# Second layer of a fused attention and two-MLP kernel in blocks of four token tiles, and a padded copy of U's columns for the shared tile

## Chip, cores and metric

One core of one Trainium2 chip. The metric is the device time in microseconds (us) of one execution; three timed runs of the kernel before gave 1811.48 us in the median (1806.88 to 1813.13). All times below are us unless marked ns.

## What is computed

Three stages on float32 data with 8 batches, 576 tokens and 512 channels. In short form:

```python
x = attention(q, k, v)              # per head, in chunks of 64 tokens
x = x + relu(layernorm(x) * g_ln @ w1_a) @ w2_a        # first layer, 512 -> 2048 -> 512
u = x + transpose(transpose(x) @ U @ V)                # along the tokens: U is 576x32, V is 32x576
out = u + relu(u @ w1_b) @ w2_b                        # second layer, 512 -> 2048 -> 512
```

The MLP matrices, U and V arrive as float64; the kernel turns them into float32 parts itself.

## The kernel before, in words

The 8 x 576 = 4608 tokens are 36 tiles of 128 (`NT`). A batch is four and a half tiles long, so every ninth tile is shared: of tiles 9k to 9k+8, the one with `r = i % 9 == 4` holds 64 tokens of batch 2k and 64 of batch 2k+1.

**Blocks and steps.** Both layers work on blocks of `TPB = 3` tiles (`BT = 384` tokens): blocks 0 to 11 are the first layer, 12 to 23 the second. A block has `NF = 16` steps, one for each slice of 128 of the 2048 hidden channels; `seq` (line 652) lists all 384 pairs (block, slice) in order. In the main loop (lines 806 to 829) step `g` issues `g1` of pair `g`, then whatever the dictionary `plan` holds for that step, then `g2` of pair `g - 2` (`LAG = 2`). Each engine executes its own instructions in that order.

**g1** (line 602) makes one slice of the hidden layer: 12 matmuls into one PSUM bank `h0` or `h1` (4 slices of the input channels, and for each the products high by high, high by low, low by high of a split number format). The weight slice, 128x128, is the stationary operand; the transposed activations `xh`, `xl` are the moving one, 384 columns wide. ScalarE writes the relu's high part `hh` (line 613), VectorE its remainder `hl` (line 614), each to a ring of three buffers.

**g2** (line 617) adds that slice into the outputs: for each tile of the block 3 matmuls, with `hh` or `hl` as stationary operand and 512 columns of `w2` moving, into the tile's own bank `acc0` to `acc2`. After the last slice `finish` (line 629) adds the residual on VectorE, and `store` writes the tiles out four steps later.

**Preparation.** While one block is computed, `plan` prepares the next. For a tile of the second layer: `u_load` (SP queue) reads the first layer's result back, `st_U` adds the low-rank part (one matmul, or two for a shared tile, and a VectorE add), `st_US` and `gather` move it through DRAM with DMAs of the ACT queue, `st_UE` transposes it on VectorE, rounds it on ScalarE (`xh`) and takes the remainder on GpSimd (`xl`). The three tiles start at offsets 0, 4 and 8 in the steps of the block before; `z_load`, `z_sum`, `z_rep` prepare a batch's low-rank factor ahead of its first tile.

**Low-rank sums.** `z_mm` (line 531) multiplies the finished tile `i` of the first layer by U's rows for it. The 32 result rows go to one of four groups of 32 PSUM partitions (`grp = r % 4`, `r = i % 9`) of the bank `z`. Line 539 lets a shared tile use 64 of its rows for one batch and the other 64 for the next, by two calls. The sums of a block's tiles are issued together, at most in two places: blocks with a shared tile issue part 0 at one step and part 1 three steps later. `ut` holds U's rows in 9 columns of tiles; its column 4 has rows 512 to 575 of U on top and rows 0 to 63 below.

**Order around the change.** U is loaded at step 27 (`load_ut`), V at step 175 (`load_vst`: 8 DMAs on SP, then conversion on ScalarE and VectorE). Block 11 runs from step 176 to 191, the second layer from step 192. During block 11 `w_back` and `w_split` replace the weights.

Of the kernel before, what the change touches and what calls it, by code (L numbers as in the profile page):

```python
# [18 lines left out]
def fused_kernel(ctx, tc, q, k, v, g_ln, w1_a, w2_a, U, V, w1_b, w2_b, out):  # L19
    nc = tc.nc  # L20
# [8 lines left out]
    TPB = 3  # L29
    BT = TPB * P  # L30
    NB = NT // TPB
    KT = DM // P
    NF = DFF // P
    LAG = 2
# [4 lines left out]
    const = ctx.enter_context(tc.tile_pool(name="const", bufs=1))  # L39
    wp = ctx.enter_context(tc.tile_pool(name="wp", bufs=1))  # L40
    rawp = ctx.enter_context(tc.tile_pool(name="rawp", bufs=3))
    xtp = ctx.enter_context(tc.tile_pool(name="xtp", bufs=2))
    hp_ = ctx.enter_context(tc.tile_pool(name="hp", bufs=3))
    xp = ctx.enter_context(tc.tile_pool(name="xp", bufs=7))
    qkp = ctx.enter_context(tc.tile_pool(name="qkp", bufs=1))
    t1 = ctx.enter_context(tc.tile_pool(name="t1", bufs=1))
# [16 lines left out]


    ident = const.tile([P, P], F32, name="ident")
    gbc = const.tile([P, DM], F32, name="gbc")
    ut = const.tile([P, 9, RK], F32, name="ut")
    nhalf = const.tile([P, 1], F32, name="nhalf")

    x1_d = [dr.tile([P, DM], F32, name=f"x1d{i}") for i in range(NT)]  # L70
# [129 lines left out]
    def load_ut():  # L200
        Ui = U.bitcast(I32)
        raw = raw_tile()
        v = raw.rearrange("p (t r) w -> p t (r w)", r=RK)
        nc.sync.dma_start(out=v[:, 0:4], in_=Ui[0:512].rearrange("(t p) r -> p t r", p=P))
        nc.sync.dma_start(out=v[0:64, 4], in_=Ui[512:576])
        nc.sync.dma_start(out=v[64:128, 4], in_=Ui[0:64])
        nc.sync.dma_start(out=v[:, 5:9], in_=Ui[64:576].rearrange("(t p) r -> p t r", p=P))
        o = ut.rearrange("p t r -> p (t r)")
        a, c = conv_f32(raw, P, 9 * RK, o)
        nc.vector.tensor_tensor(out=c, in0=c, in1=a, op=ALU.mult)  # L210
        nc.vector.tensor_tensor(out=o, in0=o, in1=c, op=ALU.add)

    def load_vst():
        Vi = V.bitcast(I32)
        vst = qkp.tile([P, S + 2 * CH], F32R, tag="kt", name="vst")
        zs["V"] = vst
        nc.gpsimd.memset(f32(vst[:, 0:CH]), 0.0)
        nc.gpsimd.memset(f32(vst[:, CH + S:]), 0.0)
        n = S // 2
        for h in range(2):  # L220
            raw = raw_tile()
            for m in range(4):
                nc.sync.dma_start(out=raw.rearrange("p a w -> p (a w)")[32 * m:32 * m + 32, :2 * n], in_=Vi[:, 2 * n * h:2 * n * (h + 1)])
            o = vst[:, CH + n * h:CH + n * (h + 1)]
            a, c = conv_f32(raw, P, n, o)
            for m in (1, 3):
                pp = slice(32 * m, 32 * m + 32)
                nc.vector.tensor_tensor(out=o[pp], in0=c[pp], in1=a[pp], op=ALU.mult)
# [239 lines left out]
    def st_N(i):  # L468
# [9 lines left out]
        else:  # L478
            nc.vector.tensor_scalar(out=xn, in0=x, scalar1=mv[:, 0:1], scalar2=rs, op0=ALU.subtract, op1=ALU.mult)  # L479
            nc.gpsimd.tensor_tensor(out=xn, in0=xn, in1=gbc, op=ALU.mult)  # L480

    def xt_tile(j, t):
        if t == 0:
            xt[j] = (xtp.tile([P, KT, BT], F32R, tag="xh", name="xh"), xtp.tile([P, KT, BT], F32R, tag="xl", name="xl"))
        return (a[:, :, t * P:(t + 1) * P] for a in xt[j])

    def st_E1(i):
        src = state.pop(("n", i)).rearrange("p (k c) -> p k c", k=KT)
# [42 lines left out]
    def z_mm(i, part):  # L531
        r = i % 9
        b = 2 * (i // 9) + part
        grp = r % 4
        first = r in ((0, 1, 2, 3) if part == 0 else (4, 5, 6, 7))
        last = r in ((4, 1, 2, 3) if part == 0 else (8, 5, 6, 7))
        if b not in zst:
            zst[b] = psp.tile([P, DM], F32, tag="z", name="zps")
        pp = slice(0, P) if r != 4 else slice(64 * part, 64 * part + 64)
        mm(zst[b][32 * grp:32 * grp + 32, :], ut[pp, r, :], xs[i][pp, :], start=first, stop=last)  # L540

    def z_out(b):
        z4 = t1.tile([P, DM], F32, tag="xn" if b == B - 1 else "cvd", name="z4")
# [27 lines left out]
    us = {}  # L571

    def u_load(i):
        x1 = xp.tile([P, DM], F32, tag="x", name="x1")
        nc.sync.dma_start(out=x1, in_=x1_d[i])
        us[i] = x1

# [15 lines left out]
        spread(NT + i, us[i])  # L593

    def st_UE(i):
        split(NB + i // TPB, i % TPB, state.pop(("w", NT + i)), "xn")


    ht = {}
    acc = {}  # L600

    def g1(j, f):
        xh, xl = xt[j]
        wh, wl = (a.rearrange("p (k f) -> p k f", k=KT) for a in wt[0, f])
        ps = ps_tile("h", [P, BT])
        n = 0
        for kk in range(KT):
            for l, r in ((wh, xh), (wh, xl), (wl, xh)):
                mm(ps, l[:, kk], r[:, kk, :], start=n == 0, stop=n == 3 * KT - 1)
                n += 1  # L610
        hi = hp_.tile([P, BT], F32R, tag="hh", name="hh")
        lo = hp_.tile([P, BT], F32R, tag="hl", name="hl")
        nc.scalar.activation(out=hi, in_=ps, func=AF.Relu)  # L613
        nc.vector.scalar_tensor_tensor(out=lo, in0=ps, scalar=0.0, in1=f32(hi), op0=ALU.max, op1=ALU.subtract)  # L614
        ht[j, f] = (hi, lo)

    def g2(j, f):
        hi, lo = ht.pop((j, f))
        wh, wl = wt[1, f]
        for t in range(TPB):  # L620
            if f == 0:
                acc[j, t] = psp.tile([P, DM], F32, tag=("h1", "m1", "z")[t] if j == 1 else f"acc{t}", name="acc")
            tt = slice(t * P, (t + 1) * P)
            a = acc[j, t]
            mm(a, hi[:, tt], wh, start=f == 0, stop=False)
            mm(a, hi[:, tt], wl, start=False, stop=False)
            mm(a, lo[:, tt], wh, start=False, stop=f == NF - 1)

    def finish(j):
        for t in range(TPB):  # L630
            i = j % NB * TPB + t
            x = xs[i] if j < NB else us[i]
            nc.vector.tensor_tensor(out=x, in0=acc.pop((j, t)), in1=x, op=ALU.add)  # L633

    def store(j):
        for t in range(TPB):
            i = j % NB * TPB + t
            if j < NB:
                nc.sync.dma_start(out=x1_d[i], in_=xs[i])
            else:  # L640
                nc.sync.dma_start(out=out[i * P:(i + 1) * P, :], in_=us.pop(i))


    with tc.manual_schedule():
# [7 lines left out]
        seq = [(0, f) for f in range(LEAD)]  # L652
        for f in range(NF):
            seq += [(1, f)] + [(0, f + LEAD)] * (f + LEAD < NF)
        seq += [(j, f) for j in range(2, 2 * NB) for f in range(NF)]
        pos = {x: n for n, x in enumerate(seq)}

        for n in range(2, 2 * NB):
            g = NF * (n - 1)
            ends = []  # L660
            for t in range(TPB):
                i = (n % NB) * TPB + t
                s = g + 4 * t
                if n == 2:
                    s = (10, 15, 24)[t]
                    at(s - 6, load_qk_nat, i)
# [39 lines left out]
            if 2 <= n < NB - 1:  # L706
                parts_ = 4 if n < 4 else 9
                for part in range(parts_):
                    at(g + {2: 12, 3: 8, 4: 4}.get(n, 3) + part, load_qk, n + 1, part, parts_)
        for n in range(2 * NB):  # L710
            g = pos[n, NF - 1] + 1
            at(g + LAG + 2, store, n)
            if n < NB:
                g = max(g, pos[1, NF - 1] + 1)
                both = any((n * TPB + t) % 9 == 4 for t in range(TPB))
                early_z = []
                for t in range(TPB):
                    i = n * TPB + t
                    r = i % 9
                    if r <= 4:  # L720
                        early_z.append((z_mm, (i, 0)))
                    if r == 4:
                        at(g + 5, z_out, 2 * (i // 9))
                    if r >= 4:
                        plan.setdefault(g + (6 if both else 3), []).insert(0, (z_mm, (i, 1)))
                    if r == 8:
                        at(g + 5, z_out, 2 * (i // 9) + 1)
                z_first[g + 3] = z_first.get(g + 3, []) + early_z
# [5 lines left out]
        for p in range(len(EARLY), NP):  # L734
            at(max(p - 4, 2), weight, p)
        at(27, load_ut)
        at(NF * (NB - 2) + 15, load_vst)
        PRE_G = 58
        for p in range(NP):
            g = PRE_G + p * 7 // 2  # L740
# [65 lines left out]
        for g in range(len(seq) + LAG + 3):  # L806
            if g < pos[1, 0] + LAG:
                banks.update(h=("h0", "m0"), m=("m1", "h1", "z"))
            elif g < 10:
                banks.update(h=("h0", "m0"), m=())  # L810
            elif g <= pos[0, NF - 1] + LAG:
                banks.update(h=("h0",), m=("m0",))
            elif g == pos[0, NF - 1] + LAG + 1:
                banks.update(h=("h0",), m=("m0", "acc1", "acc2"))
            elif g < 2 * NF:
                banks.update(h=("h0", "acc0"), m=("m0", "acc1", "acc2"))
            elif g <= 2 * NF + 1:
                banks.update(h=("h0",), m=("m0",))
            else:
                banks.update(h=("h0", "h1"), m=("m0", "m1"))  # L820
            if g < len(seq):
                g1(*seq[g])
            for fn, a in plan.get(g, ()):
                fn(*a)
            if LAG <= g < len(seq) + LAG:
                j, f = seq[g - LAG]
                g2(j, f)
                if f == NF - 1:
                    finish(j)
# [24 lines left out]
```

## Time and profile before

| what | value |
|---|---|
| median of three timed runs | 1811.48 us |
| lowest and highest | 1806.88 and 1813.13 us |
| the profiled execution's own time | 1808.26 us |
| its span in the trace | 1806.5 us |
| mean granted TensorE clock | 0.985 |
| TensorE busy with matmuls | 1747.0 us |
| DMA traffic | 167.57 MB |

The span is the time from the first to the last instruction that the trace shows; 1.8 us lie around it. PE stands for TensorE's matmuls, PEld for its weight loads, DVE for VectorE, ACT for ScalarE, POOL for GpSimd, SP for the queue that issues most DMAs. Matmuls overlap in the pipeline, so the duration of one is longer than the distance to the next; rates below are taken from distances between starts. A busy share near 100% says that the engine is never without work, not that each piece of it is as short as it can be.

### The profile page before, as it was taken

How to read it: one execution, taken by the hardware profiler on the slowest of the kernel's cores; microseconds unless marked ns; L12 is line 12 of the kernel's file. 1: busy time of each engine (PE TensorE's matmuls, PEld its weight loads, DVE VectorE, ACT ScalarE, POOL GpSimd, SP SyncE). 2: the span in 40 equal slices, each digit the busy share in tenths (PEclk: the TensorE clock that was granted, in tenths of full speed). 3: DMA queues.
4: the chain of work that ended last, by engine and by line, in shares of the span. 5: the costliest groups of instructions: out<-in, count | busy, mean ns of one | idle time of the engine just before them, and what ended most of it. 6: DMA issues, size and time to landing. Idle time of an engine off the chain costs nothing.

```text
span 1806.5 us, 26695 instructions
## 1 busy us (share of the span) xinstructions
PE 1747.0 (97%) x10536; PEld 1538.9 (85%) x10536; DVE 790.3 (44%) x1544; ACT 381.5 (21%) x714; POOL 183.3 (10%) x196
## 2 busy tenths in 40 slices
PE   6899898999999999999999999999999999999999
PEld 4778777888788888888889899999999999999998
DVE  6898643466566656556545221221221221221211
ACT  4333311122222222212124111111111111111110
POOL 1000001111011120111211001010001001010000
PEclk8899999999999999999999999999999999999999
DMA  7344324546365463554345221220221121220100
GB/s 170 100 125 109 78 70 97 131 118 155 104 149 138 110 169 108 144 149 115 110 132 175 65 65 41 65 76 24 77 70 42 59 65 41 65 76 24 53 30 18
DMA packets 293101, 167.57 MB, mean 93 GB/s; under 512 B 189424, under 2 KB 251888, under 8 KB 292976
## 3 DMA queue, kind: packets, MB, share of 16 engines
q1 hardware_dynamic: 212048, 93.48, 20.2%
q10 hardware_dynamic: 80928, 72.39, 14.1%
q8 instruction: 83, 1.36, 0.3%
q14 instruction: 42, 0.34, 0.1%
HBM read 112.82 MB, written 52.95 MB: 92 GB/s over the span
## 4 chain that ended last, share of the span: by engine, by line
PE 85%; DVE 7%; DMA 3%; issue 2%; ACT 1%; SPq 1%; POOL 1%; ACTq 0%; DVEq 0%; POOLq 0%
PE psh L59 41%; PE acc L59 40%; PE psm L59 2%; PE zps L59 1%; DVE hl L614 1%; DMA raw<-in_moe_w_ch 1%; DVE cvt L94 1%; DVE cvt L102 1%; ACT hh L613 1%; DMA k<-in_k 0%; DMA q<-in_q 0%; DMA nat<-in_k 0%; SPq L282 0%; DVE cvt L93 0%; DVE cvt L103 0%
## 5 line engine op out<-in xcount | busy, mean ns | idle before, releaser
L614 DVE SCALAR_TENSOR_TENSOR hl<-psh,hh 128x384 fp32r<-128x384 f32 x384 | 213.6, 556 | 876.0 <-ACT hh L613 875.4
L59 PE MATMUL psh<-xh,w0h 128*128 128x384 f32 x1536 | 522.1, 340 | 16.0 <-DVE hl L614 12.9
L59 PE MATMUL psh<-xh,w0l 128*128 128x384 f32 x1536 | 521.2, 339 | 1.0 <-DVE w0l L146 1.0
L59 PE MATMUL psh<-xl,w0h 128*128 128x384 f32 x1536 | 519.3, 338 | 1.1 <-DVE xl L498 0.9
L59 PE MATMUL acc<-w1h,hh 128*128 128x512 f32 x1152 | 459.2, 399 | 4.9 <-DVE x L633 4.0
L59 PE MATMUL acc<-w1l,hh 128*128 128x512 f32 x1152 | 456.2, 396 | 0.0
L59 PE MATMUL acc<-w1h,hl 128*128 128x512 f32 x1152 | 455.6, 395 | 0.0
L613 ACT ACTIVATE hh<-psh 128x384 fp32r<-128x384 f32 x384 | 188.8, 492 | 1121.9 <-PE psh L59 947.7
L59 PEld LDWEIGHTS psh<-xh,w0h 128*128 128x128 f32 x1536 | 291.4, 190 | 37.2 <-DVE hl L614 16.4
L59 PEld LDWEIGHTS psh<-xl,w0h 128*128 128x128 f32 x1536 | 290.9, 189 | 18.0 <-DVE xl L498 1.3
L59 PEld LDWEIGHTS psh<-xh,w0l 128*128 128x128 f32 x1536 | 290.6, 189 | 1.4 <-DVE w0l L146 1.4
L59 PEld LDWEIGHTS acc<-w1h,hh 128*128 128x128 f32 x1152 | 217.2, 189 | 50.3 <-ACT hh L613 7.7
L59 PEld LDWEIGHTS acc<-w1h,hl 128*128 128x128 f32 x1152 | 216.8, 188 | 48.1
L59 PEld LDWEIGHTS acc<-w1l,hh 128*128 128x128 f32 x1152 | 216.9, 188 | 36.9
L520 POOL TENSOR_TENSOR xl<-wT,xh 128x512 fp32r<-128x512 f32 x63 | 81.3, 1290 | 941.0 <-ACT xh L519 937.3
L460 POOL TENSOR_SCALAR rs<-mv 128x1 f32<-128x1 f32 x36 | 8.8, 244 | 537.6 <-DVE mv L458 529.4
L519 ACT CAST xh<-wT 128x512 fp32r<-128x512 f32 x63 | 39.4, 625 | 89.1 <-DVE wT L517 89.1
L633 DVE TENSOR_TENSOR x<-acc,x 128x512 f32<-128x512 f32 x72 | 45.2, 681 | 3.7 <-PE acc L59 3.7
L517 DVE STREAM_TRANSPOSE wT<-w 128x512 f32<-128x512 f32 x63 | 44.3, 703 | 5.6 <-DMA wd<-v_pl 2.3
L480 POOL TENSOR_TENSOR xn<-xn,gbc 128x512 f32<-128x512 f32 x27 | 35.8, 1327 | 41.9 <-DVE xn L479 34.0
L59 PEld LDWEIGHTS psm<-kt_pl,qt 64*64 64x64 f32 x1056 | 20.3, 145 | 17.5 <-issue 13.3
L59 PE MATMUL psm<-kt_pl,qt 64*64 64x64 f32 x1056 | 24.9, 237 | 8.7 <-DVE kt_pl L300 7.5
(99 smaller groups left out, 924.0 us busy)
## 6 DMA issues: line engine op xcount, KB each, us to landing
w<-sp ACTq DMA_DIRECT2D x90, 256.0 KB, 2.7
x1d<-x SPq DMA_DIRECT2D x36, 256.0 KB, 2.5
x<-x1d SPq DMA_DIRECT2D x36, 256.0 KB, 3.1
sp<-x ACTq DMA_DIRECT2D x144, 64.0 KB, 1.8
out<-x SPq DMA_DIRECT2D x36, 256.0 KB, 2.1
v_pl<-in_v SPq DMA_DIRECT2D x132, 64.0 KB, 2.8
raw<-in_moe_w_ch SPq DMA_DIRECT2D x64, 128.0 KB, 2.9
raw<-in_moe_w_ch SPq DMA_DIRECT2D x16, 512.0 KB, 3.5
```

The source lines that it names most:

```text
L59: nc.tensor.matmul(o, lhsT=l, rhs=r, start=start, stop=stop)
L94: nc.vector.scalar_tensor_tensor(out=bi, in0=hw, scalar=-0x40000000, in1=bi, op0=ALU.bitwise_and, op1=ALU.bitwise_or)
L102: nc.vector.scalar_tensor_tensor(out=c, in0=d, scalar=2.0 ** -20, in1=c, op0=ALU.mult, op1=ALU.add)
L460: nc.gpsimd.tensor_scalar(out=rs, in0=mv[:, 1:2], scalar1=1e-6, scalar2=None, op0=ALU.add)
L480: nc.gpsimd.tensor_tensor(out=xn, in0=xn, in1=gbc, op=ALU.mult)
L517: nc.vector.transpose(out=x.rearrange("p k (a j) -> p a k j", a=4), in_=w.rearrange("p a (k i) -> p a k i", k=KT))
L519: nc.scalar.copy(out=hi, in_=x)
L520: nc.gpsimd.tensor_tensor(out=lo, in0=x, in1=f32(hi), op=ALU.subtract)
L613: nc.scalar.activation(out=hi, in_=ps, func=AF.Relu)
L614: nc.vector.scalar_tensor_tensor(out=lo, in0=ps, scalar=0.0, in1=f32(hi), op0=ALU.max, op1=ALU.subtract)
L633: nc.vector.tensor_tensor(out=x, in0=acc.pop((j, t)), in1=x, op=ALU.add)
```

## The change

The second layer gets blocks of its own: `TP2 = 4` tiles, 9 blocks of 16 steps instead of 12. Its `g1` matmuls have 512 moving columns in place of 384, its `g2` runs 12 matmuls in place of 9. The fourth accumulator is the bank `m1` in the first of these blocks (in which other work then has `m0` alone) and `z` in the others. The preparation offsets are 0, 4, 6, 8. The activation buffers and the hidden rings of the first layer become parts of one tile `act`; from block 11 on the rings lie in the buffers `q6` and `k6`, which attention no longer needs. A block's fourth residual tile goes alternately to the buffers `cvd` and `gbc`.

`ut` gets a tenth column: GpSimd copies the lower half of column 4 to it and writes zeros to its upper half and to the lower half of column 4, so that both calls for a shared tile use all 128 rows. V's DMAs are issued at step 169 and its conversion at 173.

```diff
+    TP2 = 4
+    NB2 = NT // TP2
...
-    xtp = ctx.enter_context(tc.tile_pool(name="xtp", bufs=2))
-    hp_ = ctx.enter_context(tc.tile_pool(name="hp", bufs=3))
+    actp = ctx.enter_context(tc.tile_pool(name="actp", bufs=1))
...
-    gbc = const.tile([P, DM], F32, name="gbc")
-    ut = const.tile([P, 9, RK], F32, name="ut")
+    gbc = t1.tile([P, DM], F32, tag="gbc", name="gbc")
+    ut = const.tile([P, 10, RK], F32, name="ut")
...
+        nc.gpsimd.memset(ut[0:64, 9], 0.0)
+        nc.gpsimd.tensor_copy(out=ut[64:128, 9], in_=ut[64:128, 4])
+        nc.gpsimd.memset(ut[64:128, 4], 0.0)
...
+    act = actp.tile([P, 2 * 2 * KT * BT + 6 * BT], F32R, name="act")
+
+    def tiles_of(j):
+        return [j * TPB + t for t in range(TPB)] if j < NB else [(j - NB) * TP2 + t for t in range(TP2)]
...
+            n = KT * P * len(tiles_of(j))
+            o = (2 * n * ((j - NB) % 2)) if j >= NB else (2 * n + 3 * BT) * (j % 2)
+            xt[j] = tuple(act[:, o + m * n:o + (m + 1) * n].rearrange("p (k c) -> p k c", k=KT) for m in range(2))
...
+    def h_tiles(j, f):
+        n = BT if j < NB else TP2 * P
+        if j < NB - 1:
+            m = 2 * KT * BT
+            r = hpos[j, f] % 3
+            return (act[:, o + r * BT:o + (r + 1) * BT] for o in (2 * m + 3 * BT, m))
+        if not hring:
+            for nm in ("q6", "k6"):
+                hring[nm] = qkp.tile([P, 3, TP2 * P], F32R, tag=nm, name="h" + nm[0])
+        return (hring[nm][:, hpos[j, f] % 3, :n] for nm in ("q6", "k6"))
...
-        pp = slice(0, P) if r != 4 else slice(64 * part, 64 * part + 64)
-        mm(zst[b][32 * grp:32 * grp + 32, :], ut[pp, r, :], xs[i][pp, :], start=first, stop=last)
+        mm(zst[b][32 * grp:32 * grp + 32, :], ut[:, 9 if r == 4 and part else r, :], xs[i], start=first, stop=last)
...
-        x1 = xp.tile([P, DM], F32, tag="x", name="x1")
+        j, t = divmod(i, TP2)
+        x1 = xp.tile([P, DM], F32, tag="x", name="x1") if t < 3 else t1.tile([P, DM], F32, tag=("cvd", "gbc")[j % 2], name="x1")
...
-        ps = ps_tile("h", [P, BT])
+        ps = ps_tile("h", [P, len(tiles_of(j)) * P])
...
-        for t in range(TPB):
+        for t in range(len(tiles_of(j))):
             if f == 0:
-                acc[j, t] = psp.tile([P, DM], F32, tag=("h1", "m1", "z")[t] if j == 1 else f"acc{t}", name="acc")
+                tag = f"acc{t}" if t < 3 else ("m1" if j == NB else "z")
+                acc[j, t] = psp.tile([P, DM], F32, tag=("h1", "m1", "z")[t] if j == 1 else tag, name="acc")
...
-        seq += [(j, f) for j in range(2, 2 * NB) for f in range(NF)]
+        seq += [(j, f) for j in range(2, NB + NB2) for f in range(NF)]
...
-                s = g + 4 * t
+                s = g + (0, 4, 6, 8)[t]
...
-        at(NF * (NB - 2) + 15, load_vst)
+        at(NF * (NB - 2) + 9, load_V)
+        at(NF * (NB - 2) + 13, make_vst)
...
-                banks.update(h=("h0", "h1"), m=("m0", "m1"))
+                banks.update(h=("h0", "h1"), m=("m0",) if pos[NB, 0] + LAG - 1 <= g <= pos[NB, NF - 1] + LAG else ("m0", "m1"))
```

## Rows read from the trace of the kernel before

**Rows 1.** The page: busy time of the engines; shares of the chain that ended last.

```profile
PE 1747.0 (97%) x10536; PEld 1538.9 (85%) x10536; DVE 790.3 (44%) x1544; ACT 381.5 (21%) x714; POOL 183.3 (10%) x196
...
PE 85%; DVE 7%; DMA 3%; issue 2%; ACT 1%; SPq 1%; POOL 1%; ACTq 0%; DVEq 0%; POOLq 0%
```

**Rows 2.** Busy time by stretch: PE, PEld, DVE, ACT, POOL; granted clock, DMA share, GB/s.

```profile
130.00:400.00 270.00, 252.16 (x1666) 216.13 (x1665) 159.26 (x329) 64.61 (x119) 22.93 (x28) 0.97 0.41 101
400.00:900.00 500.00, 493.03 (x3560) 425.89 (x3559) 303.97 (x612) 112.56 (x207) 73.16 (x84) 1.00 0.51 132
900.00:1000.00 100.00, 99.86 (x489) 86.42 (x490) 51.74 (x86) 33.49 (x66) 11.79 (x11) 1.00 0.48 154
1000.00:1800.00 800.00, 800.00 (x4008) 723.27 (x4002) 168.34 (x293) 117.32 (x229) 65.31 (x51) 1.00 0.17 52
```

**Rows 3.** What PE waited for from 400 us on: us, times, longest.

```profile
PE psm L59 <- DVE kt_pl L300: 3.6, 2, 2.1
PE acc L59 <- DVE x L633: 2.4, 2, 1.5
```

**Rows 4.** Timeline of PE, three steps of the second layer: start, duration.

```profile
1201.97 0.33 PE L59 MATMUL psh<-xh,w0h 128*128 128x384 f32 x1
...
1203.04 0.33 PE L59 MATMUL psh<-xh,w0h 128*128 128x384 f32 x1
...
1204.08 0.39 PE L59 MATMUL acc<-w1h,hh 128*128 128x512 f32 x1
...
1206.16 0.33 PE L59 MATMUL psh<-xh,w0h 128*128 128x384 f32 x1
...
1214.53 0.33 PE L59 MATMUL psh<-xh,w0h 128*128 128x384 f32 x1
```

**Rows 5.** Timeline of PE: the last 18 matmuls, first and last of them.

```profile
1798.18 0.39 PE L59 MATMUL acc<-w1h,hh 128*128 128x512 f32 x1
...
1802.04 0.39 PE L59 MATMUL acc<-w1h,hl 128*128 128x512 f32 x1
```

**Rows 6.** Timeline of PE: two low-rank sums, one of a shared tile.

```profile
942.44 2.02 PE L59 MATMUL zps<-x,ut 128*32 128x512 f32 x4
944.39 0.50 PE L59 MATMUL psm<-zs,vst 128*128 128x512 f32 x1
```

**Rows 7.** Timeline of PE: three low-rank sums, none of a shared tile.

```profile
999.77 1.06 PE L59 MATMUL zps<-x,ut 128*32 128x512 f32 x6
1000.76 0.50 PE L59 MATMUL acc<-w1h,hh 128*128 128x512 f32 x1
```

**Rows 8.** PE's instruction groups by shape: the low-rank sums (rows, PSUM columns).

```profile
L59 PE MATMUL zps<-x,ut 128*32 128x512 f32 x64 | 15.8, 605 | 0.0
...
L59 PE MATMUL zps<-x,ut 64*32 64x512 f32 x16 | 8.3, 601 | 0.0
```

**Rows 9.** Groups of DVE, ACT and POOL between 1000 and 1800 us.

```profile
L614 DVE SCALAR_TENSOR_TENSOR hl<-psh,hh 128x384 fp32r<-128x384 f32 x189 | 105.4, 558 | 613.4 <-ACT hh L613 613.3
...
L633 DVE TENSOR_TENSOR x<-acc,x 128x512 f32<-128x512 f32 x33 | 20.6, 682 | 0.0
...
L613 ACT ACTIVATE hh<-psh 128x384 fp32r<-128x384 f32 x189 | 93.1, 493 | 628.8 <-PE psh L59 628.8
...
L520 POOL TENSOR_TENSOR xl<-wT,xh 128x512 fp32r<-128x512 f32 x33 | 42.5, 1288 | 656.0 <-ACT xh L519 656.0
```

**Rows 10.** SP's timeline around V's load: start, time taken by the issues.

```profile
871.75 2.68 SPq L282 DMA_DIRECT2D v_pl<-in_v  x4
889.39 10.53 SPq L553 DMA_DIRECT2D zr<-zd  x8
900.33 6.60 SPq L223 DMA_DIRECT2D raw<-in_moe_V  x8
```

**Rows 11.** Timeline: two halves of one tile, read and written by different engines.

```profile
546.61 0.69 PE L59 MATMUL psm<-kt_pl,qt 64*64 64x64 f32 x32
547.72 0.70 DVE L421 STREAM_TRANSPOSE kt_pl<-w 128x512 f32<-128x512 f32 x1
```

More of the change, by code (lines that the diff above doesn't have):

```diff
@@ L207, in load_ut @@
         nc.sync.dma_start(out=v[:, 5:9], in_=Ui[64:576].rearrange("(t p) r -> p t r", p=P))
-        o = ut.rearrange("p t r -> p (t r)")
+        o = ut[:, 0:9].rearrange("p t r -> p (t r)")
         a, c = conv_f32(raw, P, 9 * RK, o)
@@ L211, in load_ut, with load_V, make_vst @@
         nc.vector.tensor_tensor(out=o, in0=o, in1=c, op=ALU.add)
-    def load_vst():
-        Vi = V.bitcast(I32)
+        nc.gpsimd.memset(ut[0:64, 9], 0.0)
+        nc.gpsimd.tensor_copy(out=ut[64:128, 9], in_=ut[64:128, 4])
+        nc.gpsimd.memset(ut[64:128, 4], 0.0)
+    vraw = {}
+    def load_V():
+        Vi = V.bitcast(I32)
+        n = S // 2
+        for h in range(2):
+            vraw[h] = raw_tile()
+            for m in range(4):
+                nc.sync.dma_start(out=vraw[h].rearrange("p a w -> p (a w)")[32 * m:32 * m + 32, :2 * n], in_=Vi[:, 2 * n * h:2 * n * (h + 1)])
+    def make_vst():
         vst = qkp.tile([P, S + 2 * CH], F32R, tag="kt", name="vst")
@@ L220, in load_vst @@
         for h in range(2):
-            raw = raw_tile()
-            for m in range(4):
-                nc.sync.dma_start(out=raw.rearrange("p a w -> p (a w)")[32 * m:32 * m + 32, :2 * n], in_=Vi[:, 2 * n * h:2 * n * (h + 1)])
+            raw = vraw.pop(h)
             o = vst[:, CH + n * h:CH + n * (h + 1)]
@@ L480, in st_N @@
             nc.gpsimd.tensor_tensor(out=xn, in0=xn, in1=gbc, op=ALU.mult)
+    act = actp.tile([P, 2 * 2 * KT * BT + 6 * BT], F32R, name="act")
+    def tiles_of(j):
+        return [j * TPB + t for t in range(TPB)] if j < NB else [(j - NB) * TP2 + t for t in range(TP2)]
     def xt_tile(j, t):
         if t == 0:
-            xt[j] = (xtp.tile([P, KT, BT], F32R, tag="xh", name="xh"), xtp.tile([P, KT, BT], F32R, tag="xl", name="xl"))
+            n = KT * P * len(tiles_of(j))
+            o = (2 * n * ((j - NB) % 2)) if j >= NB else (2 * n + 3 * BT) * (j % 2)
+            xt[j] = tuple(act[:, o + m * n:o + (m + 1) * n].rearrange("p (k c) -> p k c", k=KT) for m in range(2))
         return (a[:, :, t * P:(t + 1) * P] for a in xt[j])
+    hring = {}
+    def h_tiles(j, f):
[8 more added lines that the diff above has]
+        return (hring[nm][:, hpos[j, f] % 3, :n] for nm in ("q6", "k6"))
     def st_E1(i):
@@ L595, in st_UE @@
     def st_UE(i):
-        split(NB + i // TPB, i % TPB, state.pop(("w", NT + i)), "xn")
+        split(NB + i // TP2, i % TP2, state.pop(("w", NT + i)), "xn")
     ht = {}
     acc = {}
+    hpos = {}
     def g1(j, f):
@@ L610, in g1 @@
                 n += 1
-        hi = hp_.tile([P, BT], F32R, tag="hh", name="hh")
-        lo = hp_.tile([P, BT], F32R, tag="hl", name="hl")
+        hi, lo = h_tiles(j, f)
         nc.scalar.activation(out=hi, in_=ps, func=AF.Relu)
@@ L629, in finish @@
     def finish(j):
-        for t in range(TPB):
-            i = j % NB * TPB + t
+        for t, i in enumerate(tiles_of(j)):
             x = xs[i] if j < NB else us[i]
@@ L635, in store @@
     def store(j):
-        for t in range(TPB):
-            i = j % NB * TPB + t
+        for i in tiles_of(j):
             if j < NB:
@@ L654, in fused_kernel @@
             seq += [(1, f)] + [(0, f + LEAD)] * (f + LEAD < NF)
-        seq += [(j, f) for j in range(2, 2 * NB) for f in range(NF)]
+        seq += [(j, f) for j in range(2, NB + NB2) for f in range(NF)]
         pos = {x: n for n, x in enumerate(seq)}
-        for n in range(2, 2 * NB):
+        hpos.update(pos)
+        for n in range(2, NB + NB2):
             g = NF * (n - 1)
             ends = []
-            for t in range(TPB):
-                i = (n % NB) * TPB + t
-                s = g + 4 * t
+            for t, i in enumerate(tiles_of(n)):
+                s = g + (0, 4, 6, 8)[t]
                 if n == 2:
@@ L709, in fused_kernel @@
                     at(g + {2: 12, 3: 8, 4: 4}.get(n, 3) + part, load_qk, n + 1, part, parts_)
-        for n in range(2 * NB):
+        for n in range(NB + NB2):
             g = pos[n, NF - 1] + 1
```

## Prediction

> **What bounds the kernel now.** I read the page first: TensorE has matmuls in flight for 1747.0 of the 1806.5 us span and holds 85% of the chain that ended last, while VectorE is busy for 44% of the time and ScalarE for 21% [rows 1]. The view by stretch then says where [rows 2]: from 130 to 400 us TensorE still lacks 18 of 270 us, from 400 to 900 us 7 of 500, and from 1000 us on nothing, at a granted clock of 1.00, the 2.4 GHz level. The second layer lies in that last stretch, so no wait there can be removed; only fewer or closer matmuls shorten it. The waits of TensorE from 400 us on are a few pieces of 1 to 2 us, for transposed k and for the residual adds [rows 3].
>
> Since the engine counts as busy all the time, I went to the distances between starts. Three steps take 1214.53 - 1201.97 = 12.56 us, 4.187 us each [rows 4]. In one, the 12 matmuls of 384 columns take 2.11 us (175.8 ns each), the 9 of 512 columns 2.08 us (231.1 ns). Neither is constant: the first six of the 12 take 1.07 us (178.3 ns), the last six 1.04 (173.3 ns), and the last 18 matmuls of the kernel, where no 384-column work is left, are 3.86 us / 17 = 227.1 ns apart [rows 5], 4 ns closer than the same matmuls inside a step. Between 173.3 and 227.1 ns lie 128 columns, 0.42 ns each, which is one per cycle at 2.4 GHz; what is left of either is 12 to 14 ns per matmul. I read this as follows: a stream of one width settles at its columns plus 12 to 14 ns, and a change of width costs some 4 or 5 ns more per matmul for some of the next. Why, no row shows.
>
> **The second layer.** Before: 192 steps of 21 matmuls, 192 x 4.187 = 803.9 us. After: 144 steps of 24 matmuls, all of 512 columns, so 3456 matmuls instead of 4032 with the same columns in all. What a 512-column `g1` matmul costs is not in the trace. From above: the distance of 512-column matmuls inside a step, 231.1 ns, gives 3456 x 0.2311 = 798.7, a gain of 5.2 us. From below: the settled distance, 227.1 ns, gives 784.9, a gain of 19.0 us. I take 19.0, because the widths no longer change and the rows of a single width are the nearest case; those last 18 matmuls also change bank and weights every few matmuls, so such a change alone does not unsettle the stream. The low-rank updates (line 589) keep their 40 matmuls of 512 columns.
>
> **What stands behind it.** The relu pieces get 512 columns: 493 and 558 ns [rows 9] become at most 657 and 744 ns, 1.4 us in a step of 5.45 us, and `g2` uses them two steps later. Cost 0. `finish` has four adds of 0.68 us, 2.7 us, during and after the 2.7 us of the next `g1`, and the first bank is needed only after that `g1`; if VectorE is late, the next `g2` waits. The upper bound is one add at each of 8 boundaries, 5.5 us; I take 0, since nothing is waited for after 1000 us now [rows 2]. Preparation of four tiles at offsets 0, 4, 6, 8 has two steps, 10.9 us, for each of the last three, with 1.29 us of GpSimd as its longest piece [rows 9]; the fourth tile is transposed where the third was, two steps ahead of its use. In block 11 the steps are still 4.2 us, which leaves 8.4 us after the last transposition for a chain whose longest piece is that 1.29 us. The DMA issues keep their number, 36 loads and 36 stores on SP and five per tile on the ACT queue; the fourth tile's load needs a buffer whose store is issued five steps earlier. With `m1` taken in block 12, low-rank updates share `m0`, two steps apart. Cost 0 each.
>
> **One tile for many buffers.** `act` and the hidden rings are now slices of single tiles. Would `g2` then wait for the newest write to another slice? The matmuls at 546.61 read one half of the tile `kt_pl`, and the transpose into its other half, which stands ahead of them in the program, starts only at 547.72 [rows 11]. So slices are waited for apart. Cost 0.
>
> **V, U and gbc.** V's 8 issues take 6.6 us of SP and now stand ahead of the `zr` loads, behind which the first residual and weight loads wait; SP was free from 874.4 to 889.4 [rows 10], so none is delayed. The conversion moves away from where VectorE was crowded, but TensorE idled only 0.14 us in that stretch [rows 2]: gain 0 to 0.14, and the most that a delay could cost is the 6.6 us of the issues; I take 0. U's three small GpSimd operations, each below the 1.29 us of a full tile [rows 9], end long before the first sum, and GpSimd has 23 us of work in 270 there. `gbc` only changes its place. Cost 0.
>
> **The low-rank sums.** Each sum shows as two records. Two sums, one of them of a shared tile, hold TensorE for 944.39 - 942.44 = 1.95 us [rows 6]; three sums without a shared tile take 0.99 us [rows 7]. So sums of different column groups run beside each other, but those with 64 rows (16 records [rows 8]) run alone. There are 8 groups with a shared tile. With 128 rows I take a pair to cost what three cost: 0.96 us less. At 242 us four other sums stand in the same group and the shared tile's column group is taken by tile 0, so nothing is gained; the group at 258 lies where TensorE waits for others anyway [rows 2]. Six groups remain (480, 496, 705, 722, 928 and 942 us), 6 x 0.96 = 5.8 us. The lower bound is the two after 900 us, 1.9 us, if the waits before [rows 3] grow by what is saved; the upper bound is seven groups, 6.7 us.
>
> **The sum.** 19.0 + 5.8 = 24.8 us off the profiled execution's 1808.26 us is 1783.5. That execution was 3.2 us faster than the median of the runs, 1811.48; from the median it is 1786.7, and I forecast 1787.
>
> **Rivals.**
> (a) The matmuls stay unsettled. If the addition comes from the handover between `g1` and `g2` and not from the width, 231.1 ns hold: 5.2 + 5.8 = 11.0, 1800.5 us. For it: it is the only distance seen in steps. Against: the end of the kernel. Chance 0.22.
> (b) Cost goes by columns alone. 175.8 ns x 512 / 384 = 234.4 ns for a `g1` matmul; 1728 x (0.2344 + 0.2311) = 804.4, no gain in the layer, and only the sums' 5.8 remain: 1805.7 or a little more. Against: the last six of a group, 173.3 ns, scale to 231.1, yet 227.1 is seen. Chance 0.06.
> (c) The sums don't run beside each other with padded rows: 19.0 alone, 1792.5 us. Against: all tiles that already use 128 rows do. Chance 0.08.
> (d) Slower: 512-column `g1` matmuls unsettle the stream more than 384-column ones. The slow half of a group, 178.3 ns, scales to 237.7 ns; for all 3456 that is 821.5, 17.6 us more, less 5.8: 1823.3 us. It decides from (803.9 + 5.8) / 3456 = 234.3 ns on. Against: the low-rank updates already are 512-column matmuls with other operands and stand among these without a visible price. Chance 0.04.
>
> A rule of the Trainium skill speaks against the change as (b) does: "TensorE: Matmul & The Clock Gate", Back-to-back issue gap, gives columns / 2.4 plus 2.5 ns at full clock. By it 576 fewer matmuls would bring an estimated 1.4 us in the layer, 1804.3 us with the sums. The trace shows 12 ns and more in place of 2.5.
>
> **How the numbers follow.** The forecast has 0.60, with (a) to (d) as above. A measurement of this kernel tells 0.3%, 5.4 us, from no change: the border is 1806 us. The forecast, (a) and (c) are faster; of (b) I count half as the same. With something left for waits that I cost at nothing: faster 0.89, same 0.06, slower 0.05. The range reaches from 1780 (all seven groups and the settled distance, from the runs' spread of some 3 us below the median) to 1803 ((a), with the same spread above), and takes in (c).
>
> **What would show it.** Right: 24 matmuls per step at 227 ns, steps of 5.45 us, TensorE without idle time after 1000 us, no 64-row sums, and pairs of 1 us. Wrong: distances of 231 ns or more in `g1` or `g2`; a wait of `g2` for `hl` or for a residual add; pairs still at 1.95 us; waits for k that grow after 480 us.

## The result, and the profile after

The changed kernel took 1781.18 us in the median of four runs (1779.77 to 1782.99), the kernel before 1809.86 (1806.88 to 1813.13, four runs): a ratio of 0.9842, 95% interval 0.982 to 0.9863, so 28.7 us less by the medians. The forecast was 1787 us with a range of 1780 to 1803. The profiled execution took 1782.99 us with a span of 1781.0; against the 1808.26 of the one before that is 25.3 us less, where the sum in the prediction came to 24.8. That this is so close is partly luck, as the next rows show: the second layer gave more than forecast and the stretch ahead of it less.

The page after, the lines that answer to [rows 1]:

```profile
PE 1719.9 (97%) x9960; PEld 1458.7 (82%) x9960; DVE 779.1 (44%) x1496; ACT 372.3 (21%) x666; POOL 184.1 (10%) x199
...
PE 83%; DVE 8%; DMA 3%; issue 2%; SPq 2%; ACT 1%; POOL 1%; ACTq 0%; DVEq 0%; POOLq 0%
```

There are 576 matmuls fewer (10536 - 9960), and TensorE has the same share of a shorter span. Busy shares don't show that the kernel got better; as before the change, one has to look at distances. The timeline of PE, one step of the second layer (start, duration), answers to [rows 4]:

```profile
1206.18 0.62 PE L60 MATMUL psh<-act,w0h 128*128 128x512 f32 x2
...
1208.90 0.39 PE L60 MATMUL acc<-w1h,hq 128*128 128x512 f32 x1
...
1211.62 0.62 PE L60 MATMUL psh<-act,w0h 128*128 128x512 f32 x2
```

`g1` and `g2` have 12 matmuls each and take 2.72 us each: 226.7 ns per matmul in both, and 5.44 us per step. The slow first half of a group, 178.3 ns in [rows 4] where the second half had 173.3, has no counterpart any more.

How the 25.5 us of span divide is seen from where the second layer begins and ends. The first `g1` matmul of that layer in the kernel before (its last matmul is in [rows 5]), and then both in the kernel after:

```profile
984.68 0.33 PE L59 MATMUL psh<-xh,w0h 128*128 128x384 f32 x1
```

```profile
980.34 0.61 PE L60 MATMUL psh<-act,w0h 128*128 128x512 f32 x2
...
1776.93 0.39 PE L60 MATMUL acc<-w1h,hk 128*128 128x512 f32 x1
```

The layer took 1802.04 - 984.68 = 817.4 us and now takes 1776.93 - 980.34 = 796.6: 20.8 us less. Ahead of it 4.3 us are gained, behind it 0.4, less than that end differs by between traces (4.1 to 4.9 us from the last matmul on).

Most of what is gained ahead of it comes from the low-rank sums, as the pair that answers to [rows 6] says: 0.98 us from the first sum to the next matmul, in place of 1.95, and all records have 128 rows.

```profile
938.82 1.05 PE L60 MATMUL zps<-x,ut 128*32 128x512 f32 x4
939.80 0.50 PE L60 MATMUL psm<-zs,vst 128*128 128x512 f32 x1
```

Six such pairs would be 5.8 us. The 4.3 us hold two things that are not the sums'. First, the start of a run varies; the first sums, before and after, are:

```profile
242.39 2.04 PE L59 MATMUL zps<-x,ut 128*32 128x512 f32 x10
```

```profile
243.18 1.90 PE L60 MATMUL zps<-x,ut 128*32 128x512 f32 x10
```

Counted from there, the second layer begins 742.3 us later before and 737.2 after, 5.1 us less. Second, TensorE's granted clock: in both traces it waits over 2 us for transposed k near 456 us (2.14 before, 2.34 after), and what follows that wait, before and after (columns as in [rows 2]), differs:

```profile
456.20:460.00 3.80, 3.80 (x35) 3.03 (x28) 3.31 (x6) 0.95 (x2) 1.28 (x1) 0.56 0.02 4
```

```profile
457.80:462.00 4.20, 4.20 (x47) 3.72 (x39) 2.19 (x7) 1.25 (x2) 1.30 (x1) 1.00 0.01 4
```

Before, the clock fell to 0.5, the 1.2 GHz level, for most of that stretch, with work in flight all the while; in the execution after it stayed at 1.00. From the sums at 403.37 us before and 404.79 after to the next, at 480.01 and 480.08, with no shared tile between, that is 1.35 us of the 5.1, and it belongs to these two executions: two further traces of the unaltered changed kernel have the fall too. What TensorE waited for from 400 us on shows where some of the 5.8 us went:

```profile
PE psm L60 <- DVE kt_pl L312: 4.7, 2, 2.4
PE acc L60 <- DVE x L668: 3.9, 3, 1.5
PE acc L60 <- ACT act L648: 0.9, 1, 0.9
PE psh L60 <- DVE act L649: 0.3, 1, 0.3
```

The waits for transposed k have grown from 3.6 to 4.7 us [rows 3]; the one near 608 us alone has gone from 1.5 to 2.4. (The third wait for a residual add was there before too, at 399 us, just outside the stretch, and so was the 0.9 us for ScalarE's piece, at 701 us.) The last row, at 914 us in block 11, has no counterpart in the trace before. None of them lies in the second layer. VectorE and ScalarE, the groups between 1000 and 1780 us, answer to [rows 9]:

```profile
L649 DVE SCALAR_TENSOR_TENSOR hk<-psh,hq 128x512 fp32r<-128x512 f32 x140 | 96.9, 692 | 600.1 <-ACT hq L648 600.0
L648 ACT ACTIVATE hq<-psh 128x512 fp32r<-128x512 f32 x140 | 83.8, 599 | 608.0 <-PE psh L60 608.0
...
L668 DVE TENSOR_TENSOR x<-acc,x 128x512 f32<-128x512 f32 x36 | 22.5, 683 | 4.8 <-PE acc L60 4.8
```

The relu pieces take 599 and 692 ns, below the bounds of 657 and 744, and idle before each group for 600 us of 780: nothing of the new work comes near the path.

### The profile page after: what moved, and what is told of

The parts are those of the page before. It is cut to its first block, busy times and chain, and to the rows that moved or that the text cites. A ratio compares the mean times of both kernels' runs of the same rounds, so it can differ in the third digit from the quotient of the medians.

```text
span 1781.0 us, 25335 instructions
## 1 busy us (share of the span) xinstructions
PE 1719.9 (97%) x9960; PEld 1458.7 (82%) x9960; DVE 779.1 (44%) x1496; ACT 372.3 (21%) x666; POOL 184.1 (10%) x199
## 4 chain that ended last, share of the span: by engine, by line
PE 83%; DVE 8%; DMA 3%; issue 2%; SPq 2%; ACT 1%; POOL 1%; ACTq 0%; DVEq 0%; POOLq 0%
PE psh L60 40%; PE acc L60 39%; PE psm L60 2%; DMA raw<-in_moe_w_ch 1%; PE zps L60 1%; DVE act L649 1%; DVE cvt L95 1%; DVE cvt L103 1%; SPq L294 1%; ACT act L648 1%; DMA k<-in_k 1%; SPq L267 0%; DVE cvt L104 0%; DVE bs L468 0%; DVE cvt L94 0%
## 5 line engine op out<-in xcount | busy, mean ns | idle before, releaser
L60 PE MATMUL psh<-act,w0h 128*128 128x384 f32 (+1 forms) x2688 | 756.5, 362 | 18.4 <-DVE act L649 13.0
L60 PEld LDWEIGHTS psh<-act,w0h 128*128 128x128 f32 x2688 | 503.2, 190 | 84.8 <-DVE act L649 16.3
L60 PE MATMUL psh<-act,w0l 128*128 128x384 f32 (+1 forms) x1344 | 486.8, 362 | 1.0 <-DVE w0l L147 1.0
L60 PE MATMUL acc<-w1h,act 128*128 128x512 f32 x1056 | 366.1, 401 | 4.8 <-DVE x L668 3.9
L60 PEld LDWEIGHTS psh<-act,w0l 128*128 128x128 f32 x1344 | 255.4, 190 | 23.8 <-DVE w0l L147 1.4
L60 PE MATMUL acc<-w1h,hq 128*128 128x512 f32 x624 | 243.0, 389 | 0.0
L60 PE MATMUL acc<-w1l,hq 128*128 128x512 f32 x624 | 243.0, 389 | 0.0
L60 PE MATMUL acc<-w1h,hk 128*128 128x512 f32 x624 | 242.9, 389 | 0.0
L60 PEld LDWEIGHTS acc<-w1h,act 128*128 128x128 f32 x1056 | 198.9, 188 | 51.6 <-ACT act L648 6.8
L60 PE MATMUL acc<-w1l,act 128*128 128x512 f32 x528 | 209.1, 396 | 0.0
```

The source lines that it names most:

```text
L60: nc.tensor.matmul(o, lhsT=l, rhs=r, start=start, stop=stop)
```

## The experiments

**The sums alone.** The kernel before with the padded copy and nothing else:

```diff
-        pp = slice(0, P) if r != 4 else slice(64 * part, 64 * part + 64)
-        mm(zst[b][32 * grp:32 * grp + 32, :], ut[pp, r, :], xs[i][pp, :], start=first, stop=last)
+        mm(zst[b][32 * grp:32 * grp + 32, :], ut[:, 9 if r == 4 and part else r, :], xs[i], start=first, stop=last)
```

> The kernel before with only the padded low-rank sums (tenth column of ut, all 128 rows). Theory: sums with 64 rows run alone, sums with 128 rows beside each other, so each pair with a shared tile takes about 0.99 us in place of 1.95. That removes 0.96 us at seven of eight places; the changed kernel kept 4.5 us of it up to the second layer, because a wait for transposed k near 608 us grew by 0.9 and the one place near 258 us gave less. So 4 to 5.5 us less than before, a ratio near 0.9973, and nothing in the second layer. Rival: the gain up to the second layer comes from the earlier load of V or from the new placement of buffers; then the sums alone bring 0 to 2 us.

Measured: 1804.30 us (10 runs) beside 1812.22 (21 runs), a ratio of 0.9958, interval 0.9944 to 0.9971, so 5 to 10 us less. Its timeline has the short pair:

```profile
939.53 1.05 PE L59 MATMUL zps<-x,ut 128*32 128x512 f32 x4
940.51 0.50 PE L59 MATMUL psm<-zs,vst 128*128 128x512 f32 x1
```

From the first place with sums to the last, both of which stand in the view of the sums' matmuls, this kernel takes 995.8 - 243.5 = 752.3 us and the kernel before 999.8 - 242.4 = 757.4: 5.1 us less. That is what the theory said; the timed gain of 7.9 us is larger than its upper end of 5.5, but its interval reaches down to it. The sums alone do it, without V's load or the new buffers.

**The reverse: the changed kernel with 64 rows.** The line above undone in the changed kernel, and the three GpSimd operations on `ut` taken out. This run, the one with V's load and the one with pairs in the first layer, below, were timed on one chip beside an unaltered changed kernel:

> The changed kernel itself, unaltered, for comparison on one chip with the three that follow: 1779 to 1783 us, a ratio of 0.982 to 0.986 to the kernel before.

> The changed kernel with the low-rank sums of a shared tile as before, 64 rows each and no tenth column's copies. Theory (they run alone, and the sums bring what is gained up to the second layer): 4 to 5.5 us more than the changed kernel, the pairs of sums at 1.95 us again and the second layer as long as in the changed kernel, 796.6 us from its first g1 matmul to the last matmul. Rival (the gain ahead of the second layer is V's load or the buffers): less than 2 us more.

The changed kernel took 1783.02 us again (ratio 0.9836, 0.9816 to 0.9856), the one with 64 rows 1789.57 (0.9869, 0.9852 to 0.9886): 6.6 us more, somewhat over the 4 to 5.5 that were expected. Its pair is long again:

```profile
943.09 2.02 PE L60 MATMUL zps<-x,ut 128*32 128x512 f32 x4
945.04 0.50 PE L60 MATMUL psm<-zs,vst 128*128 128x512 f32 x1
```

From the first to the last place with sums it takes 761.9 us where the changed kernel beside it takes 756.6, which is 5.3 us; from the last sums to the last matmul both take 778.4 us. So the two parts of the change don't touch each other. All traces together say the same: from the first sums to the first `g1` matmul of the second layer, three kernels with 64 rows take 742.3, 744.3 and 743.7 us (the kernel before, the one with pairs of steps in its second layer, and this one), six with 128 rows (the sums alone, three of the changed kernel, and its variants with V's load and with halves, below) 737.1 to 738.4, in the mean 5.8 us less. The Trainium skill, "TensorEngine Tiling (Array Packing)", Key Properties, says that a change of tiling mode drains the engine; the 1.95 against 0.98 us agree, though no run measured the drain by itself.

**V's load back to its place.**

```diff
-        at(NF * (NB - 2) + 9, load_V)
-        at(NF * (NB - 2) + 13, make_vst)
+        at(NF * (NB - 2) + 15, load_V)
+        at(NF * (NB - 2) + 15, make_vst)
```

> The changed kernel with V's load and its conversion back at step 175, one right after the other. The prediction costed their move at nothing: the same as the changed kernel within 0.3 us. Rival: the earlier load carries a part of the 4.5 us gained ahead of the second layer, then 1 to 4 us more.

1781.74 us, a ratio of 0.9829 (0.9812 to 0.9846) beside 0.9836 for the changed kernel: no difference that can be told, though times that spread by 4 to 7 us can't show 0.3. The traces agree: from the first sums to the second layer it takes 738.4 us, the changed kernel beside it 738.3. So nothing speaks against the cost of nothing.

**Fewer changes of width, nothing else.** In the changed kernel the widths are equal, but there are also fewer matmuls, so it doesn't separate the two. This kernel keeps three tiles, all counts and both widths, and only orders the second layer in pairs of steps, with `g1` cut into its matmuls (`g1_mm`) and the relu pieces (`g1_ev`):

```diff
+            paired = pos[NB, 0] <= g < len(seq)
+            if paired and g % 2 == 0:
+                g1(*seq[g])
+                g1_mm(*seq[g + 1])
+            elif paired:
+                g1_ev(*seq[g])
-            if g < len(seq):
+            elif g < len(seq):
                 g1(*seq[g])
```

> The kernel before, second layer still in blocks of three tiles, but its steps go in pairs: the matmuls of two g1 one after the other, then two g2. Same instructions, same counts, half as many changes between 384 and 512 columns. Theory (a change of width unsettles the stream): a step of 4.187 us is 0.067 us longer than 12 x 173.3 + 9 x 226.7 ns = 4.120 us, and half of these 192 x 0.067 = 12.9 us goes: 6.4 us less, a ratio of 0.9965; the second half of the 24 matmuls of 384 columns and all but the first nine of the 18 of 512 stand at 173.3 and 226.7 ns. Rival (only the number of matmuls counts, 13 ns each, or the additions belong to particular matmuls of a group): no change, 0.999 to 1.001. If the later remainder of the second hidden slice holds up g2, it gets slower, and TensorE shows waits for hl.

Measured: 1807.33 us (12 runs) beside 1812.22 (21), a ratio of 0.9976, interval 0.9966 to 0.9987. So it is faster, by 2 to 6 us. One pair of steps in its timeline of PE: the first `g1` matmul, the seventh, the first with 512 columns (here a low-rank update), the tenth of those, and the next pair's first.

```profile
1299.92 0.33 PE L59 MATMUL psh<-xh,w0h 128*128 128x384 f32 x1
...
1300.99 0.33 PE L59 MATMUL psh<-xh,w0h 128*128 128x384 f32 x1
...
1304.11 0.39 PE L59 MATMUL psm<-zs,vst 128*128 128x512 f32 x1
...
1306.19 0.39 PE L59 MATMUL acc<-w1h,hl 128*128 128x512 f32 x1
...
1308.46 0.33 PE L59 MATMUL psh<-xh,w0h 128*128 128x384 f32 x1
```

The first six of the 24 take 1.07 us (178 ns), the other 18 take 3.12 (173.3). The first nine of the 19 with 512 columns take 2.08 us (231 ns), the ten after them 2.27 (227.0). These are the same slow beginnings as in [rows 4], of the same length and once per pair of steps instead of twice. That excludes that only the count matters, and that the additions belong to particular operands: the seventh to twelfth `g1` matmul and the thirteenth to eighteenth stand at the same 173.3 ns, the latter being the first six of another `g1`. From the last sums to the last matmul the kernel takes 797.1 us against 802.3, 5.2 us less, of the 6.4 that were expected. The rest stands at three of its pairs, near 1125, 1327 and 1529 us, where the second `g1` starts late (the weight load of its first matmul, and the remainder on VectorE that frees its bank):

```profile
1326.81 0.56 DVE L620 SCALAR_TENSOR_TENSOR hl<-psh,hh 128x384 fp32r<-128x384 f32 x1
1327.42 0.19 PEld L59 LDWEIGHTS psh<-xh,w0h 128*128 128x128 f32 x1 [0.41 <-DVE hl L620]
```

There VectorE and ScalarE first make a piece of a low-rank factor, and each place costs 0.36 us, 1.1 us in all.

**The price of one matmul.** The changed kernel with each `g1` of the second layer as two rounds of 12 matmuls over 256 columns:

```diff
+        for h in range(2 if j >= NB else 1):
+            cc = slice(256 * h, 256 * h + 256) if j >= NB else slice(0, BT)
...
-                mm(ps, l[:, kk], r[:, kk, :], start=n == 0, stop=n == 3 * KT - 1)
+                    mm(ps[:, cc], l[:, kk], r[:, kk, cc], start=n == 0, stop=n == 3 * KT - 1)
```

> The changed kernel, but each g1 of the second layer makes its 512 columns in two halves of 256, 24 matmuls in place of 12 with the same columns in all. Theory (a settled matmul costs its columns at 2.4 GHz plus 13.3 ns): 256 columns take 120 ns, 24 x 120 = 2880 in place of 2720 ns, 144 x 0.160 = 23 us more; with the widths changing again up to 10 us on top: 1804 to 1815 us. Rival 1 (time goes by columns alone): the same as the changed kernel, 1781 us. Rival 2 (the 188 ns of a weight load can't be hidden behind a shorter matmul): 24 x 188 = 4510 ns, 1.8 us more per step, near 2040 us.

One run: 1806.08 us, within the first theory's 1804 to 1815. The timeline shows a `g1`, the first and the sixth `g2` matmul behind it, and the next `g1`:

```profile
1301.76 0.40 PE L60 MATMUL psh<-act,w0h 128*128 128x256 f32 x2
...
1304.63 0.40 PE L60 MATMUL acc<-w1h,hq 128*128 128x512 f32 x1
...
1305.80 0.39 PE L60 MATMUL acc<-w1h,hk 128*128 128x512 f32 x1
...
1307.38 0.40 PE L60 MATMUL psh<-act,w0h 128*128 128x256 f32 x2
```

24 matmuls take 2.87 us, 119.6 ns each. With 173.3 and 226.7 ns that makes three widths, 256, 384 and 512, and a straight line: 53.4 ns for each 128 columns and 13 ns on top, whatever the width. Time by columns alone, rival (b), falls. The weight loads, 188 ns each in the changed kernel and 191 here before a matmul of 256 columns, are hidden even where matmuls follow each other in 120 ns.

This kernel changes width twice a step as well, between 256 and 512 columns, and that costs less than between 384 and 512: only the first five of the 512-column matmuls are slow (1.17 us, 234 ns each; the other seven 1.58, 226 ns), the 256-column ones not at all. The step of 5.62 us is 0.02 us longer than 24 x 120 + 12 x 226.7 ns = 5.60, where it was 0.067 before. The layer, 822.5 us in place of 796.6, is 25.9 us longer: 23.0 for the count (1728 more matmuls at 13.3 ns) and 2.9 for the changes of width. So a change of width has no one price; it depends on the widths.

**Pairs in the first layer.** If a change of width costs time, the first layer, which keeps three tiles, can save it too. The same pairing in the changed kernel, for steps 64 to 191:

```diff
+            paired = 4 * NF <= g < pos[NB, 0]
```

> The changed kernel, and in blocks 4 to 11 of the first layer, which keep three tiles, the steps go in pairs: two g1, then two g2, so half as many changes between 384 and 512 columns. Theory (a change of width unsettles the stream): 128 steps x 0.067 / 2 = 4.3 us less than the changed kernel, or 2 to 3 where a wait for transposed k takes it back. Rival (only the count of matmuls matters): no change; and if the attention pieces, which keep their step but come after a longer run of TensorE, are late, up to 5 us more, with waits of g2 or of attention in the view of waits.

1782.18 us, ratio 0.9826 (0.9806 to 0.9845) beside 0.9836: not told apart from the changed kernel, so the 4.3 us, or 2 to 3, did not come. But the trace doesn't show the rival's "no change"; it shows a gain given back. By the start of the relu of step 137 the kernel stood 6.9 us ahead of an unaltered one (the one timed beside the runs of the next part), counted from step 64; at step 192 it stood 1.1 us ahead. What TensorE waited for from 350 to 1000 us, first in the unaltered kernel beside it (its two largest rows), then in the paired one:

```profile
PE psm L60 <- DVE kt_pl L312: 4.9, 2, 2.7
PE acc L60 <- DVE x L668: 3.9, 3, 1.5
```

```profile
PE psh L60 <- DVE act L655: 7.6, 4, 2.8
PE psm L60 <- DVE kt_pl L312: 0.7, 1, 0.7
```

The old waits are nearly gone and a new one stands there: `g1` waits for its PSUM bank, which the remainder on VectorE frees. That in turn waits for ScalarE, whose timeline shows why it is late in one of the four places:

```profile
725.94 4.92 ACTq L120 DMA_DIRECT2D raw<-in_moe_w_ch  x4
730.97 0.49 ACT L654 ACTIVATE act<-psh 128x384 fp32r<-128x384 f32 x1 [7.55 <-DMA k<-in_k]
```

The relu of a slice stands behind four DMA issues in ScalarE's queue, which are spread over 4.92 us, while the matmuls that need the bank have moved ahead by what the pairs gained. (The same four are spread over 4.63 us in that unaltered kernel, but TensorE doesn't wait there.) The wait of 2.3 us near 510 us has the same cause. The one of 2.1 us near 909 us has another: there the relu stands behind a cast of the low-rank factor that waits 4.0 us for GpSimd. The fourth is 0.3 us.

The waits are not all that is lost. Behind this one TensorE's granted clock was at the 1.2 GHz level (columns as in [rows 2]):

```profile
729.00:732.10 3.10, 0.30 (x2) 0.00 (x0) 0.56 (x1) 0.49 (x1) 0.00 (x0) 0.87 0.64 147
732.10:738.00 5.90, 5.90 (x46) 5.25 (x47) 1.84 (x4) 2.24 (x4) 1.23 (x1) 0.50 0.61 143
```

A wait of 2.8 us and 5.9 us at half the clock, worth an estimated 2.9 us, account for the fall from 7.5 to 2.1 us ahead between the relus of steps 138 and 140. Near 909 us it is 2.1 us and a clock of 0.68 over the next 5.3; near 510 us the clock stayed at 1.00.

**Pairs where they gained.** So I paired only the stretches in which the trace showed a gain, with an unaltered kernel on the same chip:

```diff
-            paired = 4 * NF <= g < pos[NB, 0]
+            paired = 64 <= g < 138 or 146 <= g < 154 or 160 <= g < 176
```

> The changed kernel once more, unaltered, beside the two that follow: a ratio of 0.982 to 0.986 to the kernel before.

> The changed kernel with the steps in pairs from step 64 to 137 only (blocks 4 to 7 and part of 8). Paired to the end of the first layer it ran up to 7 us ahead of the changed kernel by step 128, and new waits of g1 for the remainders took most of it back near steps 138, 155 and 177. Theory (the pairs' gain is real, the waits come where ScalarE is held by a row of DMA issues): 74 / 2 x 0.067 = 2.5 us less from the widths and up to 3 us of older waits removed: 2 to 5 us less than the changed kernel, a ratio 0.001 to 0.003 lower. Rival (later waits for k take back whatever comes before them): within 1 us of the changed kernel.

> As the kernel with pairs up to step 137, and pairs also in steps 146 to 153 and 160 to 175, where the fully paired kernel had gained. Theory: a further 12 x 0.067 = 0.8 us and up to 2 us less. Rival (waits near step 177 return, since the block change follows directly): no better than pairs up to step 137.

The unaltered kernel took 1783.03 us (0.9837, 0.9824 to 0.985), pairs up to step 137 1778.29 (0.981, 0.9797 to 0.9824), pairs in pieces 1776.55 (0.9795, 0.9782 to 0.9809). The last is 6.5 us faster than the changed kernel and 36.8 faster than the one before, and its interval doesn't touch the changed kernel's. Pairs up to step 137 are 4.7 us faster, of the 2 to 5 expected, with intervals that just meet; the further 1.7 us of the pieces lie within the spread. The gain of the pieces is larger than the (74 + 24) / 2 x 0.067 = 3.3 us of widths, because the waits for transposed k and for residual adds, 4.2 and 3.9 us in the unaltered kernel's trace, went as well; the view of waits of the best kernel, from 350 to 1000 us:

```profile
PE psh L60 <- DVE act L655: 3.6, 3, 2.0
PE psm L60 <- DVE kt_pl L312: 0.2, 1, 0.2
```

## Why the prediction was right, step by step

- **What bounds the kernel.** Right: TensorE has no wait in the second layer before or after, and what was to be gained lay in the distances between matmuls that a busy share of 100% hides.
- **The second layer.** Forecast 19.0 us, measured 20.8. The likeliest case, the settled distance at every place, is what came. The term was under-sized because starts read to 10 ns gave 227.1 ns for 226.7: 3456 x 0.4 ns is 1.4 us of the 1.8. It divides into 576 matmuls x 13 ns = 7.5 us and 192 x 0.067 = 12.9 us of changes of width, 20.4 together; the pairs show the second price and the halves the first. The price of the count is read from three widths, the one of a change of width from two orders of the same work. The prediction took the latter for 4 or 5 ns on some matmuls after any change; between 256 and 512 columns it is a third of that per step, 0.02 us in place of 0.067. Why a change of width costs anything was not found.
- **The low-rank sums.** Forecast 5.8 us, seen in pairs of traces 4.3 to 5.3, 5.8 in the mean of nine traces, and 6.6 to 7.9 by the medians of two experiments. The pair went from 1.95 to 0.98 us as costed. A sign of being wrong that the prediction named, a wait for k that grows after 480 us, did show in part, 0.9 us near 608 us; the sum didn't count it. How much of that is the change's is open, since the same wait is 1.5 to 2.0 us in the three traces with 64 rows and 1.7 to 2.7 in the six with 128. The half clock behind such a wait, 1.35 us between the two profiled executions, stood in no term.
- **What was costed at nothing.** V's move shows no cost in a run. `finish` has none, since nothing is waited for in the second layer. Preparation, banks, `act` and `gbc` were not taken apart, but the changed kernel with 64 rows has all of them and reaches the second layer 743.7 us after its first sums, between the 742.3 and 744.3 of two kernels without them. U's copies were not run apart from the sums. Block 11 may not be quite nothing: `g1` waits there for 0.2 to 1.1 us in the traces of the changed kernel and its variants without pairs, and for 0 to 0.4 in three without the new buffers.
- **Rivals.** (a), the unsettled distance, fell with 226.7 ns at every place of a step, although `g1` and `g2` still hand over to each other. (b) fell with the halves. The rule beside it, columns / 2.4 plus 2.5 ns in the Trainium skill, "TensorE: Matmul & The Clock Gate", Back-to-back issue gap, which that section gives for an isolated matmul, doesn't hold for this stream, in which each matmul has its own weight load: 13 ns in place of 2.5 at three widths. (c) fell with both experiments on the sums, (d) with the first step of the layer.
- **The number.** 1787 stood 5.8 us above the median. Of that 1.6 lie in the base, since the four runs of before that it was measured against had a median of 1809.86 and not 1811.48; the rest is the under-sized layer and the spread between runs. The lower bound of the range, 1780, was set wider than its own reasons: 1811.48 - 19.0 - 6.7 - 3 is 1782.8, and the median of 1781.18 lies under that. And 25.3 us between the profiled executions came so near to 24.8 because two errors cancel, 1.8 us too little for the layer and 1.5 too much ahead of it.

## What to carry to other kernels

When TensorE is busy all the time, divide a stretch by its matmuls and compare groups of equal shape at different places: the fastest place shows what the others could be, here 4 to 5 ns for each of the first matmuls after a change between 384 and 512 columns and 13 ns for each matmul at all. Equal widths for the two halves of the MLP were worth more here (12.9 us) than the smaller count of instructions (7.5), while in the kernel with halves the count (23.0) outweighed the changes of width (2.9). Where the widths must differ, longer runs of one width take back a part, as long as the engines that empty PSUM aren't held up by DMA issues or waiting work of their own queues. A wait of 2 us on TensorE can cost twice, if the granted clock falls behind it; look at the clock of the stretch that follows. Short sums that use only part of the rows can be slower than the same sums padded with zeros.

## What was not expected of the hardware

The slow beginning after a change between 384 and 512 columns has a fixed length, six matmuls of 384 columns or nine of 512, and the same numbers wherever it stands; a low-rank update counts as one of the nine, though it writes another bank. After 256 columns it is five of 512, and none of the 256 are slow. Waits of 2.1 to 2.8 us on TensorE were followed by 3 to 6 us at the 1.2 GHz level in some executions and not in others: 2.14 us before the change was, 2.34 and 2.39 after it were not. Executions of one program differ mainly ahead of the second layer: between runs of the changed kernel the first sums began anywhere from 240.1 to 246.9 us, while from the first `g1` matmul of the second layer to the last matmul eight traces with the same second layer agreed to 0.01 us, 796.6 us.
